# Half loads for the first batch, a fourth early tile, and a new order of the first slots in an attention and mixture-of-experts kernel

## The chip, the cores and the metric

The kernel runs on one core of a Trainium2 chip. TensorE (PE) does the matrix products, ScalarE (ACT) and VectorE (DVE) work on the results, GpSimd (POOL) does part of the element-wise work and starts the indirect transfers, and SyncE (SP) starts the other transfers. Each engine takes its instructions in the order of its own queue, and the engines meet in semaphores. The metric is the device time of one execution in microseconds (us), the median of several runs.

## The reference

Attention over eight batches with eight heads of 64: 32 global tokens that see everything, and 512 local tokens that see the global ones and a window of 32 to either side. Its output, 8 x 544 = 4352 rows of 512, goes through a layer of eight experts, of which each row uses one:

```python
s_ll = np.where(np.abs(pos[:, None] - pos[None, :]) <= 32, s_ll, -1e9)
a_l = sm(np.concatenate([s_lg, s_ll], axis=-1))       # softmax; global queries see all keys
x = attn_out.transpose(0, 2, 1, 3).reshape(4352, 512)
...
e_idx = np.argmax(x @ w_gate, axis=1)                 # one expert for each row
for e in range(8):
    h = np.maximum(x[e_idx == e] @ w1[e], 0.0)        # 512 -> 1024
    out[e_idx == e] = gate_w * eom * (h @ w2[e])      # 1024 -> 512
```

## The kernel before

**Attention.** Each batch has ten units of work: four pairs of heads times two halves of the local rows (`Local`), and two units for the global rows (`Global`) at places 4 and 7. `advance` runs them as a software pipeline: scores of one unit, transposes of the one two places earlier, and the weighted sum (`pv`) of the one three places earlier stand next to each other in the engines' queues. A half's units use the first or the second half of the queries' and keys' columns alone; the global units use all. The queries (32 + 512 columns for each pair) and keys (640 columns, with copies of the global keys between the blocks) are loaded by `load_pairs` (L121 to L125) in pairs of heads on SP's queue; for batch 0 pair 0, then pair 1, then three of the five blocks of values (`load_v`), then pairs 2 and 3, then the other two blocks. The values are split into a high and a low part (`split_v`) after the second and third unit, and `copy_v` copies some of their rows within the on-chip memory on the same SP queue. The mask comes on GpSimd's queue (L158), behind four `memset`s and the identity. Two kinds of units use it: one adds it on VectorE (L272), the other on TensorE (L261).

**Routing.** Each row tile of 128 tokens is split, transposed on SP's queue, and multiplied with the router's weights; `Router.small` then works out expert, rank and weight of each row, and the rows are written to `xd` in DRAM. After the last batch the table is made: how many tiles each expert needs (`tiles`, `cum`), which rows each slot takes (`idx`), and in `tab`, for each slot, whether the expert changes and which weights come next. A slot is 128 rows of one expert; at most NSLOT = 34 + 7 = 41 are needed.

**Early tiles.** KPRE = 3 tiles of expert 0 are taken ahead of the table, from the tokens of the first 25 row tiles (`list_pre`, `fetch_pre`, `turn_pre`). Their 48 chunks of matmuls (8 of stage 1 and 8 of stage 2 for each) are handed out by `work(n)` between the small instructions of the last routing, and `work_all` issues what is left when the table has been made. Each output goes through ScalarE (`s2_out`, L682) and by an indirect transfer on GpSimd (L683) to its rows of `out`.

**Slots.** NBASE = 36 slots always run, and `rest` runs two and three more if slot 36, and then slot 38, is in use. A slot has its rows gathered (`gather`, L1040, GpSimd) and transposed (`xtrans`, L1046, SP), then stage 1 (`stage1`, 96 matmuls of 128 x 128 x 128, L668), the rectifier and split of its result (`between`, L674 and L675, ScalarE and VectorE), stage 2 (24 matmuls of 512 columns, L679) and `store`. `run` works with stage 1 two slots ahead of stage 2. The weights w1 and w2 of an expert (2 MB each) are loaded by `fetch` (L1012, L1014, SP) under a condition from `tab`, and split into high and low halves by ScalarE and VectorE (L693 and L695 for w1). Whether a split is due is decided on the chip: `change` (L1019) and `changes` (L1028) load a flag (L994) and go through a `Switch`, whose arms are real branches of ScalarE's and VectorE's programs. An arm with no split only raises the semaphores. `changes(s)` has w2 of slot s + 1 and w1 of slot s + 3 in its charge. TensorE waits for these semaphores ahead of the next stage 1.

The order of ScalarE, VectorE, TensorE and SP is that of the program text; GpSimd's instructions are placed by a scheduler, except those called through `gp`. The first slots before the change:

```python
for s in range(2):
    change(s, 1)
    stage1(s)
    between(s)
xtrans(3)
changes(-1)
run(0, NBASE)
```

Of the kernel before, what the change touches and what calls it, by code (L numbers as in the profile page):

```python
# [25 lines left out]
P = 128  # L26
NT = NTOK // P
RPE = NT
KPRE = 3
G0, G1 = (4, 7)  # L30
LAG = 4
HK = 1
# [9 lines left out]
FI = (1, 1, 1, 2, 1, 1, 0)  # L42
PART = (0, 16, 31, NT)
NSLOT = NT + E - 1
NBASE = NSLOT - 5
XG = DM + 8
XROW = DM + 16
W = 224
# [10 lines left out]
def tile_attention_moe(  # L59
# [59 lines left out]
    w2l = [base[0][:, 2048 + 256 * f:2304 + 256 * f].bitcast(F16) for f in range(8)]  # L119


    def load_pairs(b, lo, hi):
        _, _, q, k = sets[b % 2]
        nc.sync.dma_start(q[:, lo:hi], qT[b, :, lo:hi])
        nc.sync.dma_start(k[:, lo:hi, 32:KW - 32], kT[b, :, lo:hi])  # L125

    raw = {}

    def load_v(b, i):
        raw[i] = ld.tile([P, VW], F32, name="vf", bufs=5)  # L130
        nc.sync.dma_start(raw[i], vD[b, :, i])

    def split_v(b, i):
# [9 lines left out]
    def copy_v(b, lo=0, hi=3):  # L143
        for t in sets[b % 2][0:2]:
            nc.sync.dma_start(t[0:64, 5 + lo:5 + hi], t[64:128, lo:hi])
            nc.sync.dma_start(t[64:96, 5 + lo:5 + hi], t[64:96, 4:5].broadcast_to([32, hi - lo, VW]))

    for _, _, _, k in sets:
        for lo in (0, KW - 32):
            nc.gpsimd.memset(k[:, :, lo:lo + 32], 0.0)  # L150
# [3 lines left out]
    make_identity(nc, ident)  # L154
    identb = const.tile([P, P], BF16, name="identb")
    nc.vector.tensor_copy(identb, ident)
    mask = const.tile([P, 3, W], BF16, name="mask")
    nc.gpsimd.dma_start(mask, c_mask)  # L158
    load_pairs(0, 0, 1)
    load_pairs(0, 1, 2)  # L160
    for i in (0, 4, 1):
        load_v(0, i)
    load_pairs(0, 2, 4)
    for i in (2, 3):
        load_v(0, i)
    pgbuf = [ld.tile([P, 608], F32, name=f"pgbuf{i}") for i in range(2)]
# [566 lines left out]

    def fetch_pre():
        for t in range(KPRE):
            x = ld.tile([P, XROW], F32, name="kf", bufs=3)
            gp.indirect_dma_start(out=x, out_offset=None, in_=xd[0:1 + NPRE * P, :],
                                         in_offset=bass.IndirectOffsetOnAxis(ap=ixp[:, t:t + 1], axis=0))
            pre[t] = {"x": x}
        pre_at.append(n)  # L740

    def turn_pre():
        for t in range(KPRE):
            xT = ld.tile([P, S], F32, name="qf", bufs=3).bitcast(F16)[:, 0:2 * DM].rearrange("p (k t) -> p k t", t=P)
            nc.sync.dma_start_transpose(out=xT, in_=pre[t]["x"].bitcast(F16)[:, 0:2 * DM])
            pre[t]["xT"] = xT

# [21 lines left out]

    def pre2_out(t):  # L770
        d = pre[t]
        y = ld.tile([P, VW], F32, name="vf", bufs=5)[:, 0:DM]
        s2_out(d["py"], y, d["x"])


# [290 lines left out]
    def run(lo, hi, grouped=True):  # L1066

        for s in range(lo, hi):
# [12 lines left out]
                between(s + 2)  # L1081
            store(s, grouped)

    for s in range(5):
        gather(s)
    for s in range(2):
        xtrans(s)
    fetch(-1, 1)
    fetch(-1, 2)
    xtrans(2)  # L1090
    for s in range(2):
        change(s, 1)
        stage1(s)
        between(s)
    xtrans(3)
    changes(-1)
    run(0, NBASE)

    def rest(lo, sizes):
        if not sizes:  # L1100
            return
        hi = lo + sizes[0]
        more = {e: entry(x, 3, lo) for e, x in ((ET.PE, nc.tensor), (ET.Activation, nc.scalar), (ET.DVE, nc.vector),
                                                (ET.Pool, nc.gpsimd), (ET.SP, nc.sync))}
        for arm in tc.Switch(more, 2):
            if arm == 1:
                for s in range(lo, hi):
                    gather(s)
                for s in range(lo, hi):
                    xtrans(s)  # L1110
                for s in (lo, lo + 1):
                    change(s, 1)
                    stage1(s)
                    between(s)
                if hi > lo + 2:
                    changes(lo - 1)
                else:
                    change(lo, 2)
                run(lo, hi, False)
                rest(hi, sizes[1:])  # L1120

    rest(NBASE, [2, 3])


# [72 lines left out]
```

## Time and profile before

| What | Value |
|---|---|
| Median of 3 runs | 746.26 us (745.1 to 753.59) |
| Profiled execution, device time | 746.95 us |
| Its span, first to last instruction | 745.1 us |
| TensorE busy | 686.4 us (92%) |
| VectorE, ScalarE, GpSimd busy | 51%, 51%, 32% |
| Mean granted TensorE clock | 0.974 |

The profile is of one execution. Busy time is the time in which an engine had an instruction under way. The times in the rows of the timeline count from the first instruction. `L668` is line 668 of the kernel. A `q` behind an engine's name marks its sequencer: flags, branches, semaphores and starts of transfers. The 1.9 us between device time and span lie outside the instructions.

### The profile page before, as it was taken

How to read it: one execution, taken by the hardware profiler on the slowest of the kernel's cores; microseconds unless marked ns; L12 is line 12 of the kernel's file. 1: busy time of each engine (PE TensorE's matmuls, PEld its weight loads, DVE VectorE, ACT ScalarE, POOL GpSimd, SP SyncE). 2: the span in 40 equal slices, each digit the busy share in tenths (PEclk: the TensorE clock that was granted, in tenths of full speed). 3: DMA queues.
4: the chain of work that ended last, by engine and by line, in shares of the span. 5: the costliest groups of instructions: out<-in, count | busy, mean ns of one | idle time of the engine just before them, and what ended most of it. 6: DMA issues, size and time to landing. Idle time of an engine off the chain costs nothing.

```text
span 745.1 us, 23135 instructions
## 1 busy us (share of the span) xinstructions
PE 686.4 (92%) x9042; PEld 525.4 (71%) x9042; DVE 379.4 (51%) x1110; ACT 377.3 (51%) x866; POOL 240.4 (32%) x335
## 2 busy tenths in 40 slices
PE   4999999999999989947999899999999998999991
PEld 3788887878788777647667577667776775776660
DVE  3798989898998976710333410134225251343200
ACT  3788889898899994101342411133235262243210
POOL 3335374664748464320112121111211212121110
PEclk9999999999999999978999999999999999999996
DMA  7764979678677784297548573365765978652110
GB/s 229 226 168 127 293 213 287 148 243 208 161 236 157 208 159 75 101 264 144 168 141 221 112 149 90 81 173 124 166 189 124 238 170 212 163 113 65 49 44 14
DMA packets 113797, 120.18 MB, mean 161 GB/s; under 512 B 81615, under 2 KB 83407, under 8 KB 111762
## 3 DMA queue, kind: packets, MB, share of 16 engines
q1 hardware_dynamic: 106898, 96.85, 51.2%
q0 software_dynamic: 6528, 19.67, 9.2%
q14 instruction: 295, 2.42, 1.2%
q8 instruction: 76, 1.25, 0.7%
HBM read 200.50 MB, written 19.42 MB: 295 GB/s over the span
## 4 chain that ended last, share of the span: by engine, by line
issue 47%; PE 27%; POOL 10%; DVE 8%; ACT 4%; DMA 1%; SPq 1%; POOLq 1%; DVEq 0%; ACTq 0%
PE sp L256 6%; POOL out_dram L683 5%; POOL qkv L1040 4%; PE pt L303 3%; PE pt L308 3%; PE sp L365 2%; DVE dl L324 2%; PE sp L668 1%; DMA qkv<-in_kT_dram 1%; DVE nm L267 1%; PE pt L394 1%; DVE fl L316 1%; PE sp L261 1%; PE po L421 1%; ACT qkv L709 1%
## 5 line engine op out<-in xcount | busy, mean ns | idle before, releaser
L668 PE MATMUL ph<-qkv,w1h 128*128 128x128 f16 x2304 | 203.9, 222 | 15.1 <-DMA qkv<-qkv 10.0
L668 PEld LDWEIGHTS <-w1h 128*128 128x128 f16 x2496 | 197.0, 100 | 24.0 <-issue 10.5
L668 PE MATMUL ph<-qkv,w1l 128*128 128x128 f16 x1152 | 200.8, 222 | 9.3 <-DVEq L1028 4.1
L679 PE MATMUL py<-qkv 128*128 128x512 f16 x864 | 192.0, 379 | 0.0
L675 DVE SCALAR_TENSOR_TENSOR qkv<-ph,qkv 128x512 f16<-128x512 f32 x72 | 46.8, 687 | 213.1 <-ACT qkv L674 120.6
L679 PEld LDWEIGHTS <-qkv 128*128 128x128 f16 x896 | 86.0, 98 | 97.1
L668 PEld LDWEIGHTS <-w1l 128*128 128x128 f16 x1248 | 124.2, 99 | 10.7 <-DVEq L1028 4.6
L674 ACT ACTIVATE qkv<-ph 128x512 f16<-128x512 f32 x72 | 40.0, 594 | 167.0 <-PE ph L668 103.5
L683 POOL DMA_INDIRECT out_dram<-qkv x36 | 36.4, 1011 | 208.5 <-ACT qkv L682 207.5
L1040 POOL DMA_INDIRECT qkv<-xd,idx x36 | 36.5, 1015 | 134.7 <-DMA out_dram<-qkv 131.3
L256 PE MATMUL sp<-qkv 64*128 64x224 f32 x512 | 68.6, 388 | 9.6 <-DMA qkv<-in_kT_dram 9.6
L256 PEld LDWEIGHTS sp<-qkv 64*128 64x128 f32 x512 | 45.6, 193 | 13.5 <-issue 6.3
L285 ACT ACTIVATE p<-p,nb 128x224 f32<-128x224 f32 x128 | 51.0, 474 | 7.3 <-DVE nb L272 7.2
L682 ACT ACTIVATE qkv<-py,qkv 128x512 f32<-128x512 f32 x36 | 24.8, 689 | 58.5 <-PE py L679 39.4
L324 DVE SCALAR_TENSOR_TENSOR dl<-pt,dh 128x512 f16<-128x512 f32 x80 | 53.4, 667 | 0.3
L695 DVE SCALAR_TENSOR_TENSOR w1l<-w1r,w1h 128x512 f16<-128x512 f32 x56 | 34.3, 686 | 37.4 <-ACT w1h L693 34.7
L699 ACT ACTIVATE qkv<-qkv 128x512 f16<-128x512 f32 x56 | 34.6, 629 | 32.5 <-PE py L679 31.7
L701 DVE SCALAR_TENSOR_TENSOR qkv<-qkv 128x512 f16<-128x512 f32 x56 | 34.7, 687 | 30.8 <-ACT qkv L699 21.8
L83 POOL TENSOR_TENSOR xr<-xt,xr 128x512 f16<-128x512 f32 x30 | 34.8, 1160 | 48.0 <-ACT xr L446 36.9
L272 DVE CUSTOM_DVE_ANT_0 p<-sp,mask 128x224 f32<-128x224 f32 x128 | 42.2, 385 | 15.3 <-PE sp L256 6.2
L335 PE MATMUL po<-qkv,fh 96*128 96x65 f16 x256 | 48.1, 196 | 1.1 <-DVE s L548 0.8
L312 ACT ACTIVATE fh<-pt 96x512 f16<-96x512 f32 x64 | 37.7, 589 | 22.1 <-PE pt L303 21.5
(195 smaller groups left out, 1493.5 us busy)
## 6 DMA issues: line engine op xcount, KB each, us to landing
w1r<-in_w_dram SPq DMA_DIRECT2D x38, 2048.0 KB
qkv<-in_w_dram SPq DMA_DIRECT2D x38, 2048.0 KB
vf<-in_vD_dram SPq DMA_DIRECT2D x40, 260.0 KB
qkv<-in_kT_dram SPq DMA_DIRECT2D x7, 1280.0 KB
qkv<-in_qT_dram SPq DMA_DIRECT2D x7, 1088.0 KB
xd<-xr SPq DMA_DIRECT2D x6, 1056.0 KB
qkv<-qkv SPq DMA_DIRECT2D x14, 195.0 KB
xd<-xr SPq DMA_DIRECT2D x4, 528.0 KB
```

Source lines behind the costliest of these rows:

```text
L256: nc.tensor.matmul(self.sp[:, 2 * hd + bi, 0:W], lhsT=self.q[hs, pr, qs], rhs=self.k[hs, pr, ks], start=(bi == 0 or self.fused), stop=self ...
L272: nc.vector.tensor_tensor_reduce(self.p[:, n], self.sp[:, n, 0:W], mask[:, self.half + n % 2], -0.125, 3e38, ALU.add, ALU.min, self.nb[:, ...
L285: nc.scalar.activation(self.p[:, n], src, AF.Exp, bias=self.nb[:, n:n + 1], scale=sc)
L312: nc.scalar.mul(self.fh[0:96], self.pF[0:96], PS)
L324: nc.vector.scalar_tensor_tensor(self.dl, self.pD, PS, self.dh, ALU.mult, ALU.subtract)
L335: nc.tensor.matmul(o, lhsT=fh, rhs=self.vh[0:96, 4 + i, hc], start=True, stop=False)
L668: nc.tensor.matmul(o, lhsT=w[:, k], rhs=xT[:, x], start=(n == 0), stop=(n == 11))
L674: nc.scalar.activation(hh[:, gs], v, AF.Relu)
L675: nc.vector.scalar_tensor_tensor(hl[:, gs], v, 0.0, hh[:, gs], ALU.max, ALU.subtract)
L679: nc.tensor.matmul(py, lhsT=h[:, f], rhs=w, start=(f == 0 and n == 0), stop=(f == 7 and n == 2))
L683: i = nc.gpsimd.indirect_dma_start(out=out[:, :], out_offset=bass.IndirectOffsetOnAxis(ap=x[:, XG:XG + 1].bitcast(U32), axis=0), in_=y, in ...
L1040: nc.gpsimd.indirect_dma_start(out=xs, out_offset=None, in_=xd[:, :], in_offset=bass.IndirectOffsetOnAxis(ap=idx[:, s + 1:s + 2], axis=0))
```

## The change

There are three parts.

1. The mask's load becomes GpSimd's first instruction. Batch 0's queries and keys are loaded in halves of their columns: the first halves of pair 0, pair 1 and pairs 2 and 3 (288 of 544 query columns, 352 of 640 key columns), then three blocks of values, then the second halves of all pairs in one load each, then the other two blocks.
2. KPRE becomes 4, and NBASE becomes 41 - 6 = 35, with two further groups of 3 in `rest`. The rows of the early tiles take buffers of the ring `vf` (five, used before for values and then for early outputs), which are made 528 columns wide; their transposed forms take four buffers of `qf`.
3. `begin` sets the order of the first slots: `change(1)` stands ahead of `between(0)`, and `changes(-1)` ahead of `between(1)`. Slot 2's transpose stands ahead of the first two weight loads.

```diff
-KPRE = 3
+KPRE = 4
-NBASE = NSLOT - 5
+NBASE = NSLOT - 6
...
-    def load_pairs(b, lo, hi):
+    def load_pairs(b, lo, hi, half=None):
+
         _, _, q, k = sets[b % 2]
-        nc.sync.dma_start(q[:, lo:hi], qT[b, :, lo:hi])
-        nc.sync.dma_start(k[:, lo:hi, 32:KW - 32], kT[b, :, lo:hi])
+        a, z = (0, SG + SL) if half is None else ((0, SG + 256), (SG + 256, SG + SL))[half]
+        nc.sync.dma_start(q[:, lo:hi, a:z], qT[b, :, lo:hi, a:z])
+        a, z = (0, KW - 64) if half is None else ((0, 352), (352, KW - 64))[half]
+        nc.sync.dma_start(k[:, lo:hi, 32 + a:32 + z], kT[b, :, lo:hi, a:z])
...
+    mask = const.tile([P, 3, W], BF16, name="mask")
+    nc.gpsimd.dma_start(mask, c_mask)
     for _, _, _, k in sets:
...
-    mask = const.tile([P, 3, W], BF16, name="mask")
-    nc.gpsimd.dma_start(mask, c_mask)
-    load_pairs(0, 0, 1)
-    load_pairs(0, 1, 2)
+    load_pairs(0, 0, 1, 0)
+    load_pairs(0, 1, 2, 0)
+    load_pairs(0, 2, 4, 0)
     for i in (0, 4, 1):
         load_v(0, i)
-    load_pairs(0, 2, 4)
+    load_pairs(0, 0, 4, 1)
...
-            x = ld.tile([P, XROW], F32, name="kf", bufs=3)
+            x = ld.tile([P, XROW], F32, name="vf", bufs=5)
...
-            xT = ld.tile([P, S], F32, name="qf", bufs=3).bitcast(F16)[:, 0:2 * DM].rearrange("p (k t) -> p k t", t=P)
+            xT = ld.tile([P, S], F32, name="qf", bufs=KPRE).bitcast(F16)[:, 0:2 * DM].rearrange("p (k t) -> p k t", t=P)
...
+    def begin(lo, more=True):
+
+        change(lo, 1)
+        stage1(lo)
+        change(lo + 1, 1)
+        between(lo)
+        stage1(lo + 1)
+        if lo == 0:
+            xtrans(3)
+        if more:
+            changes(lo - 1)
+        else:
+            change(lo, 2)
+        between(lo + 1)
+
     for s in range(5):
         gather(s)
-    for s in range(2):
+    for s in range(3):
         xtrans(s)
     fetch(-1, 1)
     fetch(-1, 2)
-    xtrans(2)
-    for s in range(2):
-        change(s, 1)
-        stage1(s)
-        between(s)
-    xtrans(3)
-    changes(-1)
+    begin(0)
     run(0, NBASE)
...
-    rest(NBASE, [2, 3])
+    rest(NBASE, [3, 3])
```

More of the change, by code (lines that the diff above doesn't have):

```diff
@@ L119, in tile_attention_moe @@
     w2l = [base[0][:, 2048 + 256 * f:2304 + 256 * f].bitcast(F16) for f in range(8)]
-    def load_pairs(b, lo, hi):
+    def load_pairs(b, lo, hi, half=None):
         _, _, q, k = sets[b % 2]
-        nc.sync.dma_start(q[:, lo:hi], qT[b, :, lo:hi])
-        nc.sync.dma_start(k[:, lo:hi, 32:KW - 32], kT[b, :, lo:hi])
+        a, z = (0, SG + SL) if half is None else ((0, SG + 256), (SG + 256, SG + SL))[half]
+        nc.sync.dma_start(q[:, lo:hi, a:z], qT[b, :, lo:hi, a:z])
+        a, z = (0, KW - 64) if half is None else ((0, 352), (352, KW - 64))[half]
+        nc.sync.dma_start(k[:, lo:hi, 32 + a:32 + z], kT[b, :, lo:hi, a:z])
     raw = {}
     def load_v(b, i):
-        raw[i] = ld.tile([P, VW], F32, name="vf", bufs=5)
+        raw[i] = ld.tile([P, XROW], F32, name="vf", bufs=5)[:, 0:VW]
         nc.sync.dma_start(raw[i], vD[b, :, i])
@@ L771, in pre2_out @@
         d = pre[t]
-        y = ld.tile([P, VW], F32, name="vf", bufs=5)[:, 0:DM]
+        y = ld.tile([P, XROW], F32, name="vf", bufs=5)[:, 0:DM]
         s2_out(d["py"], y, d["x"])
@@ L1110, in rest @@
                     xtrans(s)
[L1111 to L1118, printed above, removed]
+                begin(lo, hi > lo + 2)
                 run(lo, hi, False)
                 rest(hi, sizes[1:])
-    rest(NBASE, [2, 3])
+    rest(NBASE, [3, 3])
 def _constants():
```

## The prediction

> **What bounds the kernel now.** I read the page first, then stretches of time around the change of phase, then TensorE's timeline, and last the sequencers of the engines that it waited for.
>
> ```profile
> span 745.1 us, 23135 instructions
> PE   4999999999999989947999899999999998999991
> L675 DVE SCALAR_TENSOR_TENSOR qkv<-ph,qkv 128x512 f16<-128x512 f32 x72 | 46.8, 687 | 213.1 <-ACT qkv L674 120.6
> L1040 POOL DMA_INDIRECT qkv<-xd,idx x36 | 36.5, 1015 | 134.7 <-DMA out_dram<-qkv 131.3
> ```
>
> TensorE is full in nearly all forty slices (18.6 us each). The exceptions are the first slice, the slices around 316 to 350 us, and the last. The gather runs 36 times, so 36 slots of the base list are worked, and `rest` is not entered.
>
> ```profile
> core 0: us, PE busy (x) PEld busy (x) DVE busy (x) ACT busy (x) POOL busy (x), PEclk, DMA share, GB/s
> 316.60:326.60 10.00, 0.00 (x2) 0.03 (x2) 0.93 (x6) 0.69 (x1) 5.59 (x6) 0.71 1.01 180
> 326.60:334.24 7.64, 7.63 (x96) 7.46 (x96) 0.69 (x1) 0.60 (x1) 0.00 (x0) 0.71 0.99 356
> 345.69:353.83 8.14, 8.14 (x96) 8.08 (x97) 0.00 (x0) 1.12 (x3) 0.00 (x0) 0.64 0.25 41
> 353.83:364.37 10.54, 10.54 (x123) 7.71 (x121) 6.19 (x10) 4.80 (x10) 1.00 (x1) 1.00 0.41 136
> ```
>
> The columns after the stretch are its length, each engine's busy time, the granted clock, and DMA. Between the phases TensorE stands still for 10.0 us, and the next stage 1 takes 7.64 us at a granted clock of 0.71. The last row is one slot at full clock, stage 2 and the next stage 1: 10.54 us, all of it TensorE.
>
> ```profile
> 316.22 0.38 PE L679 MATMUL pt<-qkv,hl 128*128 128x512 f16 x1
> 326.60 0.37 PE L668 MATMUL ph<-qkv,w1h 128*128 128x128 f16 x2 [10.00 <-DMA qkv<-qkv]
> 335.64 0.28 PE L668 MATMUL ph<-qkv,w1h 128*128 128x128 f16 x2 [1.40 <-ACTq L1019]
> 336.51 0.23 PE L668 MATMUL ph<-qkv,w1l 128*128 128x128 f16 x1 [0.59 <-DVEq L1019]
> 345.69 0.40 PE L668 MATMUL ph<-qkv,w1h 128*128 128x128 f16 x2 [3.75 <-ACTq L1028]
> 353.83 5.34 PE L679 MATMUL py<-qkv 128*128 128x512 f16 x24
> 364.37 0.38 PE L679 MATMUL py<-qkv 128*128 128x512 f16 x1
> ```
>
> Start, length, instruction, and in brackets the idle time with its end. The early tiles end at 316.60. Stage 1 of slot 0 waits until 326.60 for its transposed rows. Stage 1 of slots 1 and 2 start at 335.64 and 345.69, each after a wait on a `Switch` (L1019 in `change`, L1028 in `changes`) that ScalarE and VectorE go through. The first stage 2 starts at 353.83. I count the gain of the middle at that point, since from there one slot follows the other.
>
> **A slot becomes an early tile.** I counted the reference's routing on its inputs: 665, 280, 1086, 535, 312, 321, 617 and 536 tokens, with 596 of expert 0 in the first 25 row tiles. With three early tiles (384 rows) the rest needs 3+3+9+5+3+3+5+5 = 36 slots, as the x36 shows. With four (512 rows, all filled from the 596) expert 0 needs 2, so 35, which is the new NBASE exactly. One slot goes: **-10.54**. The same matmuls come back as 16 chunks after the 48 that are there; the table's instructions stay between the same chunk numbers, so the new work runs at the end, in the hole of 10.00 us. TensorE is done with it at 316.60 + 10.54 = 327.1 where it idled until 326.60. VectorE gets one more `hl` (0.69 us, the 687 ns of L675) ahead of the table's last fields; SP waits for its rows then, so I cost it at nothing.
>
> The fourth tile also adds a fetch on GpSimd and a transpose on SP's queue during the last batch:
>
> ```profile
> 264.63 1.13 POOL L83 DMA_INDIRECT kf<-xd,ixp  x1 [0.17 <-DVE rc L298]
> 268.12 5.14 SPq L745 DMA_TRANSPOSE qf<-kf  x3
> L668 PE MATMUL sp<-qf,w1h x192: 216/219/221, 277.3 to 304.3; 128*128 128x128 f16 x192
> ```
>
> That is about 1.1 us on GpSimd and 5.14 / 3 = 1.7 us on SP. The early tiles are first used at 277.3, and the router's transposes behind it feed TensorE only four units later. I take 0, with bounds 0 and +1.7.
>
> **The new order at the first slots.** What stands ahead of slot 0's stage 1 on ScalarE changes: the output of the last early tile now comes at 327.3 instead of 316.64, and ScalarE's `change(0)` is queued behind it. The prices are in these rows, the last three views being instructions of ScalarE's sequencer (start in us at the end):
>
> ```profile
> 316.64 0.69 ACT L682 ACTIVATE vf<-pt,kf 128x512 f32<-128x512 f32 x1 [5.91 <-PE pt L679]
> 334.27 0.60 ACT L674 ACTIVATE qkv<-ph 128x512 f16<-128x512 f32 x1 [2.03 <-PE ph L668]
> 352.71 4.27 ACT L693 ACTIVATE w1h<-w1r 128x512 f16<-128x512 f32 x8 [10.14 <-PE ph L668]
> 353.83 4.91 DVE L695 SCALAR_TENSOR_TENSOR w1l<-w1r,w1h 128x512 f16<-128x512 f32 x8 [10.01 <-ACT w1h L693]
> L994 ACTq TENSOR_LOAD <-tab x1: 285/285/285, 334.3 to 334.3; - x1
> L1019 ACTq EVENT_SEMAPHORE  x1: 17/17/17, 335.6 to 335.6; - x1
> L994 ACTq TENSOR_LOAD <-tab x1: 287/287/287, 342.0 to 342.0; - x1
> L1028 ACTq EVENT_SEMAPHORE  x1: 17/17/17, 345.6 to 345.6; - x1
> L994 ACTq TENSOR_LOAD <-tab x1: 288/288/288, 348.7 to 348.7; - x1
> ```
>
> A `Switch` costs 1.3 us from the load of its flag to the semaphore in its arm (334.3 to 335.6) or 3.6 (342.0 to 345.6), and 3.1 more to get out to the next load (345.6 to 348.7). With the short price, stage 1 of slot 0 starts at 327.3 + 1.3 = 328.6; I take 329.0 (the wait below included) and 334.3 for its end: stage 1 feeds as many columns as stage 2 (96 x 128 = 24 x 512), so half a slot, 5.3 us at full clock. `change(1)` now stands ahead of slot 0's results: 329 + 3.1 + 1.3 = 333.4, or 335.7 with the long price, so stage 1 of slot 1 starts at some 334.7 and ends at 340.0. The 2.0 us of wait at 334.24 mostly go.
>
> Then `changes(-1)`, ahead of slot 1's results, does real work for the first time: slot 2 is now expert 1's first, so w1 has to be split there. ScalarE leaves `change(1)` at 336.5 to 338.8, does slot 0's results (0.6 until the last has started), goes through the third `Switch` (338.4 to 343.0), and 1.12 + 0.69 us later the first pair of pieces is ready: 340.2 to 344.8. The pieces follow at 4.91 / 8 = 0.61 us, faster than stage 1 uses them (5.3 / 8 = 0.66). I take 341.5, nearer the short end because both L1019 rows were short; then the first stage 2 starts at 346.8 against 353.83: **-7.0**. The bounds are -10.8 (TensorE never waits: 327.1 + 3 x 5.3 = 343.0) and 0 (341.5 becomes 345.7 and the clock falls again).
>
> Two things behind this:
>
> ```profile
> 315.12 1.01 POOL L1040 DMA_INDIRECT qkv<-xd,idx  x1 [1.92 <-issue]
> 320.19 1.01 POOL L683 DMA_INDIRECT out_dram<-vf,kf  x1 [0.30 <-issue]
> out_dram<-vf,kf POOLq DMA_INDIRECT x3, 3.9
> 318.60 4.86 SPq L1046 DMA_TRANSPOSE qkv<-qkv  x2
> 325.55 0.42 SPq L1012 DMA_DIRECT2D w1r<-in_w_dram  x1
> 327.98 10.12 SPq L1046 DMA_TRANSPOSE qkv<-qkv  x1
> ```
>
> The fourth early output reuses the buffer of the third tile's rows, which the third store still reads; that store can be issued at some 322.9 and lands 3.9 us later, at 326.8, or later under load. I cost it at 0.4, with bounds 0 and 2. On SP, slot 2's transpose moves ahead of the two weight loads: it no longer sits 10.12 us behind them, and they start some 3.5 us later than 325.55. Before, both loads (4 MB) were through the queue at 338.1, so now at 341.6 at the latest; w1 is the first of the two, so I expect it before 338, ahead of the split.
>
> **The start.**
>
> ```profile
> 8.76 0.39 DVE L272 CUSTOM_DVE_ANT_0 p<-sp,mask 128x224 f32<-128x224 f32 x1 [5.74 <-DMA mask<-in_c_mask_dram]
> 8.92 1.87 PE L256 MATMUL sp<-qkv 64*128 64x224 f32 x8 [2.70 <-DMA qkv<-in_kT_dram]
> 14.05 1.86 PE L256 MATMUL sp<-qkv 64*128 64x224 f32 x8 [2.50 <-DMA qkv<-in_kT_dram]
> 16.91 0.54 SPq L146 DMA_DIRECT2D qkv<-qkv  x1
> 19.89 0.20 PE L335 MATMUL po<-qkv,fh 96*128 96x65 f16 x1
> 2.00:6.00 4.00, 1.64 (x8) 1.27 (x8) 0.40 (x1) 0.01 (x1) 2.57 (x18) 1.00 0.94 267
> ```
>
> The first units wait for the mask until 8.76 and for keys until 8.92 and 14.05; by the shapes the third unit's keys come at the end of 3.1 MB. By halves they come at the end of 1.28 MB, some 5 us at 267 GB/s, so keys and mask come in time. But the same bytes have to arrive before the copies of the values (issued until 16.91), which queue behind the halves and gate the first weighted sum at 19.89. I take **-2.0**, with bounds 0 (the copies come no sooner) and -5.2 (both key waits, 2.70 + 2.50, carried to the end). A rule speaks against this part: the Trainium skill (DMA: Bandwidth & Descriptors, Measured) wants DMAs of at least 1 MiB and gives 138 GB/s at 64 KB. Pieces of 144 to 352 KB would by it load more slowly, and the term would be 0; the loads of the first pair, 272 and 320 KB by their shapes, make the 267 GB/s above, well over its low figure.
>
> **Sum:** -10.5 - 7.0 - 2.0 = -19.5. The profiled execution took 746.95 us (span 745.1), 0.7 over the median of 746.26; against the median this gives 746.26 - 19.5 = **727**. A measurement of this kernel can tell about 2% (14.9 us) from no change.
>
> **The rivals.**
> (a) No new wait: the `Switch` chain runs under TensorE's work. For it speak the short L1019 rows, against it the 3.6 us of L1028. -10.5 - 10.8 - 2.0 gives 723. By the Trainium skill (Advanced Engine Details and Errata, Control Flow Timing) a compare-and-branch takes about 108 ns, which would favour this; the 3.6 us row disagrees, and Runtime: NRT & Kernel Launch, Instruction fetch mechanics, says that a taken branch out of the fetched window stalls for a fetch, with which that row agrees.
> (b) The new waits take the gap's place: three dispatches at the long price, or w1 late, so the first stage 2 stays at 353.8. Only the slot and the start are won: 746.3 - 12.5 = 734.
> (c) Slower: GpSimd's order puts the gathers behind the store of the fourth tile. That store ends at about 329.3; from gather to first matmul it takes 326.60 - 315.12 = 11.5 us, so slot 0 starts at 340.8, 14.2 late: -10.5 - 2.0 + 14.2 gives 748. It decides as soon as slot 0's gather is behind that store. Against it: before, four gathers went ahead of the third store (320.19).
> (d) The change doesn't do what it says: 36 slots are still needed and `rest` is entered. 35 + 3 slots, two more than before (+21.1), and a new fill of 11.5 give over 770. By the counts no expert is nearer to another slot than 24 tokens.
>
> **How the numbers follow.** My forecast has 0.55, (a) 0.20, (b) 0.19, (c) 0.04, (d) 0.02. The range of 719.5 to 736 holds the forecast and (a) with the start's bounds (723 less 3.2) and (b) with the 1.7 us of the last batch; what it leaves out is (c), (d) and the edges, about 0.1. Faster by over 2% (under 731.3) is the forecast but for 0.02, (a), and 0.02 of (b): 0.75. Slower is (d) and a worse (c): 0.03. The rest, 0.22, is within 2%.
>
> **What would show it.** Right: 35 gathers in slots and four early stores; no 10 us hole at the phase change, a granted clock of 1.0 through the first stage 1; the first stage 2 some 30 us after the old end of the early tiles, with w1's split ending its waits; slot 0 released by ScalarE's `Switch`. Wrong: a wait over 5 us at stage 1 of slot 2 on the load of w1; a gather behind the fourth store; the first weighted sum no earlier than 19.9; or a lasting loss in the last batch.

## The result, and the profile after

| What | Before | After |
|---|---|---|
| Median of 20 runs each | 746.67 us (741.57 to 754.49) | 742.75 us (737.4 to 747.17) |
| Profiled execution: device time, span | 746.95, 745.1 us | 737.4, 735.6 us |
| End of the early tiles on TensorE | 316.60 us | 325.20 us |
| Start of the first stage 2 | 353.83 us | 358.32 us |

The time after is 0.9945 of the time before (95% interval 0.9924 to 0.9966): some 4 us won where the forecast was 19.5. The profiled execution of the changed kernel happens to be the fastest of its twenty, so the 9.5 us between the two profiles aren't the gain.

From the page of the changed kernel (span, TensorE's busy tenths, and two groups):

```profile
span 735.6 us, 23090 instructions
PE   6999999999999989994999999999999998999991
L679 DVE SCALAR_TENSOR_TENSOR qkv<-ph,qkv 128x512 f16<-128x512 f32 x70 | 45.3, 686 | 206.9 <-issue 104.7
L1044 POOL DMA_INDIRECT qkv<-xd,idx x35 | 35.2, 1007 | 134.5 <-DMA out_dram<-qkv 131.0
```

35 gathers: one slot is gone, and `rest` isn't entered. TensorE's dip at the change of phase is one slice later and as deep, and it is narrower: a single 4 where 4, 7 and 8 stood. By stretches of time, cut at the ends of TensorE's waits (length, busy time of each engine, granted clock, DMA):

```profile
core 0: us, PE busy (x) PEld busy (x) DVE busy (x) ACT busy (x) POOL busy (x), PEclk, DMA share, GB/s
325.20:326.88 1.68, 0.00 (x1) 0.00 (x1) 0.00 (x0) 0.69 (x1) 0.62 (x1) 1.00 0.94 255
326.88:338.67 11.79, 5.53 (x96) 5.36 (x96) 0.00 (x0) 0.00 (x0) 0.36 (x1) 0.88 1.04 360
338.67:348.75 10.08, 7.37 (x96) 7.20 (x97) 1.29 (x2) 1.77 (x4) 0.00 (x0) 0.81 0.63 107
348.75:358.32 9.57, 8.38 (x96) 8.21 (x97) 6.19 (x10) 5.15 (x10) 0.00 (x0) 0.64 0.27 85
```

The hole of 10.00 us is down to 1.68. But three stages 1, which would be 16 us of work at full clock, take from 326.88 to 358.32, 31.4 us (before 27.2, from 326.60 to 353.83). 10.2 of these are waits, and 21.3 are TensorE's own work: stage 1 takes 5.53 us in the second row, but 7.37 and 8.38 in the last two, where the granted clock is 0.81 and 0.64. In the second row TensorE works for 5.53 of 11.79 us while ScalarE and VectorE have nothing under way at all. TensorE's timeline names what it waited for:

```profile
326.88 0.29 PE L672 MATMUL ph<-qkv,w1h 128*128 128x128 f16 x2 [1.68 <-ACTq L1023]
338.67 0.39 PE L672 MATMUL ph<-qkv,w1h 128*128 128x128 f16 x2 [6.26 <-ACTq L1023]
348.75 0.29 PE L672 MATMUL ph<-qkv,w1h 128*128 128x128 f16 x2 [2.71 <-ACT w1h L697]
350.23 0.29 PE L672 MATMUL ph<-qkv,w1l 128*128 128x128 f16 x1 [1.19 <-DVE w1l L699]
```

The first row is a wait that was forecast (there 1.5 to 1.9 us, here 1.68). The second is new: 6.26 us ahead of slot 1's stage 1, on the `Switch` of `change(1)` (L1023). ScalarE's sequencer shows why. These are single instructions in order of time, start in us at the end of each row. L998 loads a dispatch's flag, the hint stands at the entry of the arm, L678 is slot 0's results, and the last row is `changes(-1)` at the entry of the arm that splits w1:

```profile
L998 ACTq TENSOR_LOAD <-tab x1: 468/468/468, 325.3 to 325.3; - x1
L1023 ACTq EVENT_SEMAPHORE  x1: 17/17/17, 326.8 to 326.8; - x1
L998 ACTq TENSOR_LOAD <-tab x1: 283/283/283, 333.6 to 333.6; - x1
L1023 ACTq BRANCH_PREFETCH_HINT  x1: 35/35/35, 338.5 to 338.5; - x1
L1023 ACTq EVENT_SEMAPHORE  x1: 17/17/17, 338.6 to 338.6; - x1
L678 ACTq EVENT_SEMAPHORE  x1: 38/38/38, 344.3 to 344.3; - x1
L998 ACTq TENSOR_LOAD <-tab x1: 289/289/289, 344.5 to 344.5; - x1
L1032 ACTq BRANCH_PREFETCH_HINT  x1: 35/35/35, 347.8 to 347.8; - x1
```

The first dispatch takes 1.5 us to its semaphore (325.3 to 326.8), and then 6.8 until the next load (333.6). The second takes 5.0 (333.6 to 338.6) and 5.7 to get out (344.3). The third takes 3.3 to its arm (344.5 to 347.8). In nearly all of these 22.5 us ScalarE does no work: it is on its way from one place of its program to another.

The start of the kernel did better than forecast. Mask-using unit, second unit's scores and first weighted sum of the changed kernel:

```profile
5.83 0.39 DVE L276 CUSTOM_DVE_ANT_0 p<-sp,mask 128x224 f32<-128x224 f32 x1 [2.23 <-PE sp L260]
6.25 1.86 PE L260 MATMUL sp<-qkv 64*128 64x224 f32 x8 [0.46 <-DMA qkv<-in_kT_dram]
16.94 0.20 PE L339 MATMUL po<-qkv,fh 96*128 96x65 f16 x1
```

They stood at 8.76, 8.92 and 19.89: the first weighted sum is 2.95 us earlier. This is no chance of two profiles: in the eleven profiles of this case with the half loads it comes at 16.83 to 18.26, in the three without (before, e6, e11) at 19.89 to 21.65. Part of it is lost again ahead of the phase change. The same stretch of the program, of before and then of after (columns as above):

```profile
255.00:316.60 61.60, 57.22 (x845) 43.78 (x845) 44.41 (x190) 33.40 (x79) 32.86 (x46) 0.97 0.53 118
```

```profile
252.20:325.20 73.00, 67.70 (x965) 51.39 (x965) 48.34 (x197) 35.33 (x82) 39.55 (x53) 0.98 0.62 132
```

TensorE's idle time in it is 61.60 - 57.22 = 4.38 us before and 73.00 - 67.70 = 5.30 after.

### The profile page after: what moved, and what is told of

It is laid out like the page before. It is cut to its first block, busy times and chain, and to the rows that moved or that the text cites. A ratio compares the mean times of both kernels' runs of the same rounds, so it can differ in the third digit from the quotient of the medians.

```text
span 735.6 us, 23090 instructions
## 1 busy us (share of the span) xinstructions
PE 684.9 (93%) x9042; PEld 523.6 (71%) x9042; DVE 380.9 (52%) x1110; ACT 375.7 (51%) x866; POOL 241.2 (33%) x336
## 4 chain that ended last, share of the span: by engine, by line
issue 47%; PE 24%; POOL 11%; DVE 9%; ACT 3%; DMA 2%; POOLq 1%; SPq 0%; DVEq 0%; ACTq 0%
PE sp L260 5%; POOL out_dram L687 5%; POOL qkv L1044 4%; PE pt L307 3%; PE pt L312 2%; DMA xT<-xr 2%; DVE dl L328 1%; PE sp L369 1%; DVE nm L271 1%; PE sp L672 1%; DVE fl L320 1%; POOL qkv L83 1%; PE pt L398 1%; PE sp L265 1%; PE po L425 1%
## 5 line engine op out<-in xcount | busy, mean ns | idle before, releaser
L672 PE MATMUL ph<-qkv,w1h 128*128 128x128 f16 x2240 | 196.8, 222 | 10.9 <-ACTq L1023 7.9
L672 PE MATMUL ph<-qkv,w1l 128*128 128x128 f16 x1120 | 193.9, 222 | 7.5 <-DVE w1l L699 3.4
L683 PE MATMUL py<-qkv 128*128 128x512 f16 x840 | 186.7, 379 | 0.0
L679 DVE SCALAR_TENSOR_TENSOR qkv<-ph,qkv 128x512 f16<-128x512 f32 x70 | 45.3, 686 | 206.9 <-issue 104.7
L683 PEld LDWEIGHTS <-qkv 128*128 128x128 f16 x872 | 83.8, 98 | 94.3
L678 ACT ACTIVATE qkv<-ph 128x512 f16<-128x512 f32 x70 | 38.7, 594 | 148.6 <-PE ph L672 76.9
L703 ACT ACTIVATE qkv<-qkv 128x512 f16<-128x512 f32 x56 | 32.8, 624 | 36.1 <-PE py L683 26.3
L341 PE MATMUL po<-qkv,fl 96*128 96x65 f16 x256 | 48.0, 193 | 0.5 <-DVE fl L320 0.5
```

The lines of the kernel that those rows point to most:

```text
L341: nc.tensor.matmul(o, lhsT=fl, rhs=self.vh[0:96, 4 + i, hc], start=False, stop=False)
L672: nc.tensor.matmul(o, lhsT=w[:, k], rhs=xT[:, x], start=(n == 0), stop=(n == 11))
L678: nc.scalar.activation(hh[:, gs], v, AF.Relu)
L679: nc.vector.scalar_tensor_tensor(hl[:, gs], v, 0.0, hh[:, gs], ALU.max, ALU.subtract)
L683: nc.tensor.matmul(py, lhsT=h[:, f], rhs=w, start=(f == 0 and n == 0), stop=(f == 7 and n == 2))
```

## The experiments

**Theories.** T1: the time went into ScalarE's chain of dispatches, in which each jump costs several us; before, the 10 us hole had covered the first of them. T2: it went into the order of `begin`, which puts `change(1)` ahead of slot 0's results. T3: the weights' streams (4 MB) are what delays the chain, by w1 arriving late or by slowing ScalarE's way. All ratios are to the kernel before on the same chip, with 95% intervals; "gap" is the time from the end of the early tiles to the first stage 2 in the profiled execution (before 37.2, after 33.1).

| Run | Median us | Ratio | Early tiles end | First stage 2 | Gap |
|---|---|---|---|---|---|
| e1 changed kernel again | 741.73 | 0.9883 (0.9838 to 0.9928) | 325.71 | 354.69 | 29.0 |
| e2 old order, four tiles | 744.55 | 0.9936 (0.9883 to 0.9988) | 326.44 | 360.32 | 33.9 |
| e3 no dispatch for slots 0, 1 | 733.1 | 0.9768 (0.9724 to 0.9812) | 326.13 | 346.39 | 20.3 |
| e4 w2's load late | 740.32 | 0.9874 (0.9824 to 0.9923) | 325.54 | 351.48 | 25.9 |
| e5 start only | 744.45 | 0.9955 (0.9925 to 0.9984) | 313.60 | 351.97 | 38.4 |
| e6 order only, three tiles | 743.1 | 0.9953 (0.9923 to 0.9984) | 317.28 | 349.19 | 31.9 |
| e7 first dispatch earlier | 736.8 | 0.9875 (0.9842 to 0.9909) | 325.69 | 353.52 | 27.8 |
| e8 that, and w2 late | 735.97 | 0.9889 (0.9845 to 0.9933) | 326.51 | 349.42 | 22.9 |
| e9 first dispatch twice | 750.38 | 1.0031 (0.9995 to 1.0068) | 324.71 | 363.41 | 38.7 |
| e10 e8, and w1 ahead of transposes | 739.57 | 0.989 (0.9818 to 0.9962) | 325.60 | 350.81 | 25.2 |
| e11 kernel before again | 749.26 | one run | 315.41 | 350.32 | 34.9 |
| e12 two slots for expert 0 | 735.46 | 0.9799 (0.9747 to 0.9851) | 326.96 | 348.61 | 21.6 |

**e1: the changed kernel again**, no edit.

> The changed kernel once more, for a second profile and a ratio on the chip of the runs below. Its profile had the early tiles end at 325.2 and the first stage 2 start at 358.3, 33.1 us later (before: 316.6 and 353.8, 37.2 later). Theory A (ScalarE goes through three dispatches in a row after the last early output, and each stalls for the fetch of its code): again 30 to 36 us between the two, with two or three waits of TensorE on L1023 and the split of w1 in it. Theory D (the profile was a lucky execution and the gain is lost somewhere else): that distance is near 33 but another stretch is longer by some 5 us. Ratio to the kernel before 0.99 to 1.00 by both.

The first stage 2 came at 354.69, 3.6 us sooner than in the first profile: slot 1's wait is 5.78 and slot 2's 0.69. The second dispatch's way out took 4.4 us here, 5.7 there. The gap of 29.0 us is just under the 30 to 36 that were expected. Of the 4.1 us between the two gaps, 1.75 come ahead of slot 2's stage 1 and 2.39 in it: it took 7.18 us here at a granted clock of 1.00, 9.57 there at 0.64. So one kernel's gap varies by some 4 us.

**e2: the old order of the first slots with four early tiles.**

```diff
-    for s in range(3):
-        xtrans(s)
+    for s in range(2):
+        xtrans(s)
     fetch(-1, 1)
     fetch(-1, 2)
-    begin(0)
+    xtrans(2)
+    for s in range(2):
+        change(s, 1)
+        stage1(s)
+        between(s)
+    xtrans(3)
+    changes(-1)
```

> The changed kernel with the order of the first slots of before: slot 2's transpose behind the weight loads, change(1) behind slot 0's results, changes(-1) behind slot 1's. The fourth early tile and the half loads stay. Theory A: the dispatches are the same three and stand on ScalarE one after the other in both orders, so the first stage 2 comes 30 to 36 us after the early tiles' end, within 3 us of the changed kernel, and the time is within 0.5% of it. Rival B (the new order itself costs the gain, by putting dispatches ahead of results that TensorE's next stage waits for nothing of): the distance falls to 25 us or less and the time by 8 us.

The gap is 33.9 us, against 33.1 and 29.0 with the new order, and the ratio's interval overlaps that of the change. T2 falls: with four tiles the chain begins only when the last early output is out, in either order, and the order has little say.

**e3: no dispatch ahead of the first two slots.** It leaves out the test whether w1 has to be split before slots 0 and 1; their loads stay.

```diff
-        change(lo, 1)
+        (change if lo else fetch)(lo, 1)
         stage1(lo)
-        change(lo + 1, 1)
+        (change if lo else fetch)(lo + 1, 1)
```

> The changed kernel without the two dispatches of change(0) and change(1): the test whether w1 has to be split ahead of slots 0 and 1 is left out (with these inputs it is never due); their conditional loads stay. Theory A: TensorE starts stage 1 of slot 0 when its rows are there, slot 1 follows without a wait, and only changes(-1) is left, so the first stage 2 comes 22 to 26 us after the early tiles' end instead of 33, and the time falls by 7 to 11 us against the changed kernel. Rival C (w1's arrival sets the first split): the distance stays at 31 to 35 us and the time within 2 us.

TensorE's timeline of e3:

```profile
326.96 0.27 PE L672 MATMUL ph<-qkv,w1h 128*128 128x128 f16 x2 [0.83 <-ACT vf L686]
339.70 0.28 PE L672 MATMUL ph<-qkv,w1h 128*128 128x128 f16 x2 [1.87 <-ACT w1h L697]
341.13 0.23 PE L672 MATMUL ph<-qkv,w1l 128*128 128x128 f16 x1 [1.15 <-DVE w1l L699]
346.39 5.34 PE L683 MATMUL py<-qkv 128*128 128x512 f16 x24
```

The three stages 1 by stretches of time (columns as above):

```profile
326.96:339.70 12.74, 10.88 (x192) 10.70 (x192) 1.38 (x2) 1.88 (x4) 0.99 (x1) 1.00 1.07 383
339.70:346.39 6.69, 5.54 (x96) 5.37 (x97) 4.92 (x9) 4.68 (x9) 0.00 (x0) 1.00 0.49 56
```

Behind a first wait of 0.83 us slots 0 and 1 run through. TensorE's work in the three stages 1 is 16.4 us, at a granted clock of 1.00, where it was 21.3. The first stage 2 comes 20.3 us after the early tiles: sooner than the 22 to 26 that were expected, and near the 19.7 of the forecast (346.8 less 327.1), which had the two dispatches at a short price. The time falls by 8.6 us against e1 on the same chip (741.73 to 733.1). T1 holds as far as taking away can show it.

**e4: w2's first load behind slot 3's transpose**, so that 2 MB instead of 4 stream during the chain.

```diff
             xtrans(3)
+            fetch(-1, 2)
...
     fetch(-1, 1)
-    fetch(-1, 2)
```

> The changed kernel with the first load of w2 (2 MB) moved on SP's queue from ahead of the first slots to behind slot 3's transpose. Theory A1 (the dispatches are slow because the code they fetch stands behind 4 MB of weights): the ways out of the arms, 6.7 and 5.7 us in the profile of the changed kernel, and the branch of change(1), 4.1 us, fall to about 3 us each at least for those after some 332 us, so the distance from the early tiles' end to the first stage 2 falls from 33 to 26 to 30 us. Theory A2 (a dispatch costs what it costs, whatever is being moved): 32 to 35 us, and the time within 1 us of the changed kernel.

The second dispatch went faster (branch 3.3 us, way out 3.0; e1: 4.4 and 4.4), the first dispatch's way out did not (5.8, e1 6.1). It ran beside w1's stream here too, so this doesn't speak against T3; the second one's price and the gap of 25.9 us are about what was expected if the streams slow the jumps. But the ratio can't be told from e1's, and a gap varies by some 4 us. So w2's stream is at most a part of the loss.

**e5 and e6: one part alone on the kernel before.** e5 has the mask first and the halves; e6 has the new order with three tiles and 36 slots.

> The kernel before with the first part of the change alone: the mask first, batch 0's queries and keys by halves. In the profile of the changed kernel each unit of the attention started 2.8 to 3.0 us sooner than before up to the last batch. If that comes from this part and lasts, the first weighted sum comes at 17 to 18 us instead of 19.9, the early tiles end at 313.5 to 315 instead of 316.6, and the time falls by 2 to 3 us (ratio 0.996 to 0.997). Rival: the gain is taken back in the last batch or at the table; then the early tiles end at 316 to 317 and the time stays.

> The kernel before (three early tiles, 36 slots, whole loads) with the new order of the first slots alone. Theory A (ScalarE's chain of dispatches is what counts, and it begins with the last early output): with three tiles the chain begins at 316.6, so change(0) and change(1) fall into the hole of 10 us and under stage 1 of slot 0; the waits on L1019 ahead of slot 1 go, the one on L1028 ahead of slot 2 shrinks to under 2 us, and the first stage 2 starts at 345 to 348 instead of 353.8: 5 to 9 us saved. Rival B (the new order by itself is no gain): the first stage 2 starts at 352 to 356 and the time stays within 2 us.

Each is worth about 0.5%, some 3.4 us, by itself: together 0.9%, if they add up, which no run shows; that is between the 0.55% of the whole change's twenty runs and the 1.2% of e1. So the removed slot, 10.54 us of TensorE, shows up almost nowhere in the total. e6 says why, with three tiles:

```profile
325.87 0.37 PE L668 MATMUL ph<-qkv,w1h 128*128 128x128 f16 x2 [8.59 <-DMA qkv<-qkv]
341.63 0.28 PE L668 MATMUL ph<-qkv,w1h 128*128 128x128 f16 x2 [3.64 <-ACTq L1028]
349.19 5.34 PE L679 MATMUL py<-qkv 128*128 128x512 f16 x24
```

Here stage 1 of slots 0 and 1 run in one go. ScalarE went through `change(0)` and on to `change(1)` in the 8.59 us in which TensorE waited for its rows. The hole that the fourth tile fills wasn't free: it held the first dispatch's way out. Even so e6 missed what was expected of it: 349.19 instead of 345 to 348, and some 4 us of time (743.1 against 747.05) instead of 5 to 9, for the third dispatch still made slot 2 wait 3.64 us.

**e7 and e8: the first dispatch moved into the early tiles.** `change(0)` and w1's first load go ahead of the last 15 early chunks (one more buffer in `vf`); e8 also has e4's edit.

```diff
-    work_all()
-    att.close()
+    work(49 - nwork[0])
...
     fetch(-1, 1)
+    change(0, 1)
+    work_all()
+    att.close()
     fetch(-1, 2)
     begin(0)
```

> The changed kernel with change(0) and w1's first load moved ahead of the last 15 chunks of the early tiles (all of the fourth tile's stage 2 and most of the third's), so that ScalarE's first dispatch runs while TensorE works on them, and with six buffers in the ring vf. All tests stay. Theory A: TensorE starts slot 0 without a wait on a dispatch, change(1) follows right after the last early output, and the first stage 2 comes 20 to 26 us after the early tiles' end instead of 29 to 33; the time falls by 4 to 9 us against the changed kernel. Rival (the dispatches' place doesn't matter, their number does): 28 us or more, the time within 2 us.

> e7 with w2's first load behind slot 3's transpose, as in e4. Theory A1 (code fetches wait behind the weights): a further 1 to 3 us between the early tiles' end and the first stage 2. Theory A2: the same as e7 within 1 us.

Both beat the kernel before by a little over 1%. e7's interval lies below that of the change's twenty runs, e8's overlaps it, and neither can be told from e1's. e7's gap of 27.8 us missed the expected 20 to 26 and isn't clear of e1's 29.0; e8's of 22.9 is 4.9 shorter again, where 1 to 3 were expected. In e7 TensorE lost much of the lead again:

```profile
332.64 0.28 PE L672 MATMUL ph<-qkv,w1h 128*128 128x128 f16 x2 [0.66 <-ACTq L1019]
346.20 0.40 PE L672 MATMUL ph<-qkv,w1h 128*128 128x128 f16 x2 [7.05 <-ACT w1h L697]
```

The split of w1 waits for the semaphore of slot 1's conditional load. That load is skipped, but it has its place on SP's queue, and SP reached it only at 345.3, behind slot 0's skipped load (341.6) and w2's (343.2). ScalarE stood at that semaphore from 342.2 to 345.4: 3.2 of the 7.05 us. For the rest of them it was still on its jumps. In e8, with w2 out of the way, slot 2 waits 3.76 us.

**e9: the first dispatch twice.** The opposite of e3: one more `Switch` of the same flag, with its empty arm.

```diff
-        fetch(s, which)
+        if twice:
+            change(s, which)
+        else:
+            fetch(s, which)
...
-        change(lo, 1)
+        change(lo, 1, lo == 0)
```

> The changed kernel with the dispatch of slot 0 (load of the flag, Switch with an empty arm taken) issued twice, one behind the other; nothing else is added. Theory (the gap before the first stage 2 is ScalarE's chain of dispatches, each some 1.5 us from flag to semaphore and 4 to 7 us on the way out): the first stage 2 starts 5 to 9 us after the changed kernel's 354.7 to 358.3, at 360 to 366, and the time goes up by the same 5 to 9 us, to 747 to 751. Rival (the dispatches only look long because ScalarE waits in them for w1, so that one more of them hides in the same wait): the first stage 2 stays at 354 to 359 and the time within 2 us of the changed kernel's.

```profile
338.00 0.39 PE L672 MATMUL ph<-qkv,w1h 128*128 128x128 f16 x2 [13.29 <-ACTq L1023]
346.58 0.28 PE L672 MATMUL ph<-qkv,w1h 128*128 128x128 f16 x2 [0.48 <-ACTq L1023]
355.13 0.29 PE L672 MATMUL ph<-qkv,w1h 128*128 128x128 f16 x2 [3.02 <-ACT w1h L697]
```

One empty dispatch more, and slot 0 waits 13.29 us instead of 1.68; the first stage 2 comes at 363.41, 5.1 to 8.7 later than with one, and the whole gain of the change is gone. With e3 this settles T1: taken away or doubled, the time follows the dispatches.

**e10: w1's load ahead of the first three transposes**, on e8.

```diff
+    fetch(-1, 1)
     for s in range(3):
         xtrans(s)
-    fetch(-1, 1)
     change(0, 1)
```

> The version with the first dispatch ahead of the last early chunks and w2's load late, and with w1's first load now also ahead of the three transposes of the first slots. Theory 1 (the loads of skipped experts and w1's split wait for w1's arrival at 338.9 in that version, and the stream slows ScalarE's way out): w1 arrives by 333, the first stage 2 starts at 345 to 347 instead of 349.4, and the time is 2 to 4 us under that version's 735.97. Theory 2 (ScalarE's two remaining dispatches alone set it, at the same price without the stream): the first stage 2 stays at 349 to 350 and the time within 1 us. Rival (the transposes queue behind 2 MB): slot 0's rows come after the end of the early tiles, TensorE waits for them by a DMA, and the first stage 2 comes later than 351.

```profile
332.09 0.37 PE L672 MATMUL ph<-qkv,w1h 128*128 128x128 f16 x2 [6.49 <-DMA qkv<-qkv]
345.56 0.23 PE L672 MATMUL ph<-qkv,w1l 128*128 128x128 f16 x1 [0.55 <-DVE w1l L699]
350.81 5.34 PE L683 MATMUL py<-qkv 128*128 128x512 f16 x24
```

w1 was there by 332.8, as hoped, but slot 0's rows queued behind it: the rival's DMA wait of 6.49 us. Its price would have put the first stage 2 behind 351; it came at 350.81, for ScalarE got its dispatches done in that wait, and slot 2 waited 0.55 us only. The way out of the second dispatch still took 6.1 us, though w1 was there; the DMA queues still moved 158 GB/s in its first 2.5 us. The ratio is the same as e8's.

**e11: the kernel before again**, no edit.

> The kernel before again, for a second profile. If the parts that the prediction took from one profile are steady, the early tiles end at 316 to 317, the first stage 2 starts at 353 to 355, and ScalarE's ways out of its first three dispatches are again 4.4, 5.4 and 3.0 us. If the way out varies from one execution to the next by more than 1.5 us, the first stage 2 moves with it, and a price read from one row was not safe even for the kernel before.

The ways out of the first three dispatches took 4.3, 5.5 and 3.0 us, within 0.1 of the first profile's 4.4, 5.4 and 3.0. They aren't that steady in general: e5, which changes the start alone, has 5.2, 5.6 and 3.0. The first stage 2 came at 350.32, sooner than the expected 353 to 355, for the early tiles ended 1.2 us earlier, slot 0's rows came 0.9 faster, and the third dispatch's branch took 1.6 instead of 2.8. From there to the end of the last stage 2 it took 380.17 us, in the first profile 374.83: this later stretch moves by 5 us between executions of one kernel, and by 9.8 in the two profiles of the changed one (360.79 and 370.58).

**e12: two slots for expert 0, whatever it has left.** The whole computation. The table gives expert 0 at least two slots, so slots 0 and 1 never need a split, and their dispatches and conditional loads leave the program. NSLOT is 43 for the worst case, the base list still 35.

```diff
-NSLOT = NT + E - 1
-NBASE = NSLOT - 6
+NSLOT = NT + E + 1
+NBASE = NSLOT - 8
...
     red(tiles, gt, axis=AX.X, op=ALU.add)
+    ts(tiles[:, 0:1], tiles[:, 0:1], 2.0, None, op0=ALU.max)
...
-        change(lo, 1)
+        if lo:
+            change(lo, 1)
         stage1(lo)
-        change(lo + 1, 1)
+        if lo:
+            change(lo + 1, 1)
...
-    rest(NBASE, [3, 3])
+    rest(NBASE, [3, 5])
```

and e4's edit.

> The whole computation, with no dispatch ahead of the first two slots: the table now always gives expert 0 two slots, whether it has rows for them or not, so slots 0 and 1 can never need a split of w1, and the Switches and conditional loads of slots 0 and 1 are left out of the program (NSLOT becomes 43 for the worst case; the base list stays at 35 slots, for here expert 0 needs two anyway). w2's first load stands behind slot 3's transpose. Theory (ScalarE's dispatches one behind the other are what the changed kernel lost): stage 1 of slots 0 and 1 follow the early tiles without a wait on ScalarE's sequencer, the first stage 2 starts at 345 to 347 and 18 to 21 us after the early tiles, as in the version without those dispatches, and the time is 731 to 735, at 0.975 to 0.982 of the kernel before. Rival (that version gained by something else, such as the missing work at the semaphores, or the loads that it still issued): the first stage 2 comes after 350 and the time stays at 738 to 743.

```profile
327.79 0.27 PE L672 MATMUL ph<-qkv,w1h 128*128 128x128 f16 x2 [0.82 <-ACT vf L686]
340.94 0.28 PE L672 MATMUL ph<-qkv,w1h 128*128 128x128 f16 x2 [2.27 <-ACT w1h L697]
341.72 0.23 PE L672 MATMUL ph<-qkv,w1l 128*128 128x128 f16 x1 [0.50 <-DVE w1l L699]
348.61 5.34 PE L683 MATMUL py<-qkv 128*128 128x512 f16 x24
```

The dispatches' waits are gone, as in e3, at 0.9799 (0.9747 to 0.9851) of the kernel before: this version is faster than the kernel before. Its interval lies wholly below that of the changed kernel's twenty runs; at its upper end it overlaps e1's, and e4's, which has one of its two edits. The first stage 2 missed its expectation by 1.6 us, because the one dispatch that is left took 6.7 us from its flag to its arm:

```profile
L999 ACTq TENSOR_LOAD <-tab x1: 475/475/475, 333.4 to 333.4; - x1
L1033 ACTq BRANCH_PREFETCH_HINT  x1: 46/46/46, 340.1 to 340.1; - x1
```

## Why the prediction was wrong

**A slot becomes an early tile: right in itself.** 35 slots, 16 more early chunks, no hole of 10 us, slot 0 released by ScalarE's `Switch` at 326.88 (forecast 328.6 to 329.0, which is 326.7 to 327.1 with the early tiles done 1.9 us sooner than taken). From the first stage 2 to the end of the last one, four profiles with 36 slots take 374.83 to 380.17 us, mean 376.4; the ten with 35 take 360.79 to 370.58, mean 367.5. That is 8.9 for the 10.54 of the forecast, with single profiles up to 6.8 us from their mean.

**The fourth output's buffer: 0 instead of 0.4.** The output began at 325.29, 0.09 after its last matmul.

**The start: better than forecast.** -2.95 at the first weighted sum instead of -2.0, within the bounds; 1.4 to 1.9 us of it are left where the early tiles end (325.71 and 325.20 for the forecast's 327.1). By halves the second unit waited 0.46 us for keys, where it had waited 2.70 (8.92 to 6.25 in start); the smaller pieces didn't cost the time that the prediction set against this part. By the rule of the Trainium skill that it weighed (DMA: Bandwidth & Descriptors, Measured) nothing would have been won; the measured 2.95 us decides. The fourth tile's load on the last batch was taken as 0 with an upper bound of 1.7; the 0.9 us of idle time above is of that size, though no run took the tile's fetch and transpose alone. e5 by itself gave 0.45%, about 3.4 us.

**The new order at the first slots: the step that failed.** The forecast was -7.0 at the first stage 2; the two profiles of the changed kernel have +0.9 and +4.5 (354.69 and 358.32 against 353.83), outside the stated bounds of -10.8 to 0. They hold the start's gain too, which the forecast counts by itself: from the end of the early tiles the forecast has 19.7 us to the first stage 2 and the profiles 29.0 and 33.1, so that the term alone is +2.3 and +6.4. That is 9.3 to 13.4 of the 15.8 us by which 727 missed 742.75. The mis-sized terms are the dispatches' prices: "A `Switch` costs 1.3 us from the load of its flag to the semaphore in its arm", "and 3.1 more to get out to the next load", with the short price taken "because both L1019 rows were short".

| Step of the chain | Forecast us | Measured, after | Measured, e1 |
|---|---|---|---|
| `change(0)`: flag to semaphore | 1.3 | 1.5 | 1.7 |
| its way out | 3.1 | 6.8 | 6.1 |
| `change(1)`: flag to semaphore | 1.3 to 3.6 | 5.0 | 5.2 |
| its way out | 3.1 | 5.7 | 4.4 |
| `changes(-1)`: flag to arm | 1.3 to 3.6 | 3.3 | 3.2 |
| Stage 1 of slot 2 | 5.3 | 9.6 | 7.2 |

The last row is a second term that came out too small: it was counted at full clock and with no wait for the pieces. In the changed kernel's first profile it ran at a granted clock of 0.64 and waited 1.19 us for a piece, in e1 at 1.00 with a wait of 1.64. The prediction had the clock's fall in its bound alone.

The trace of before had the warning, in rows that the prediction didn't use. The first dispatch there, of ScalarE's sequencer, the wait for slot 0's results that comes next, and slot 1's results behind the second dispatch:

```profile
L1019 ACTq EVENT_SEMAPHORE  x1: 17/17/17, 318.7 to 318.7; - x1
L674 ACTq EVENT_SEMAPHORE  x1: 8486/8486/8486, 323.1 to 323.1; - x1
L674 ACT ACTIVATE qkv<-ph x2: 597/597/597, 341.0 to 342.0; 128x512 f16<-128x512 f32 x2
```

The way out took 4.4 us, and the second one, from 335.6 to slot 1's results at 341.0 (the last row), up to 5.4; 3.1 was one of the shortest of that trace. Of the 23 ways out from an empty arm there that end at a load or a semaphore, eleven take 2.9 to 3.6 us and twelve 4.1 to 8.8, mean 4.5. They can be sorted by what the DMA queues move meanwhile. These are the first 2.5 us of two ways out of before, of the first two of the changed kernel, and of the second one of e4 (GB/s in the last column):

```profile
345.68:348.18 2.50, 2.50 (x24) 2.44 (x25) 0.00 (x0) 0.00 (x0) 0.00 (x0) 0.50 0.05 13
518.26:520.76 2.50, 2.50 (x17) 1.21 (x15) 0.00 (x0) 0.00 (x0) 0.59 (x1) 1.00 0.87 312
326.89:329.39 2.50, 2.50 (x45) 2.50 (x46) 0.00 (x0) 0.00 (x0) 0.35 (x1) 1.00 1.09 242
338.68:341.18 2.50, 2.50 (x24) 2.50 (x25) 0.00 (x0) 0.00 (x0) 0.00 (x0) 0.50 0.80 278
337.30:339.80 2.50, 2.50 (x29) 2.50 (x30) 0.00 (x0) 0.00 (x0) 0.00 (x0) 0.61 0.02 7
```

They took 3.0, 6.2, 6.7, 5.7 and 3.0 us. Of the 23 of before, the nine at up to 126 GB/s took 2.9 to 3.1 us, the seven at 312 and more 5.6 to 6.5, and those between 3.3 to 8.8; in the changed kernel the fourteen at up to 163 GB/s took 2.8 to 4.1, the eight at 242 and more 5.7 to 7.3. The first row is the one from which the prediction took its 3.1. It read the price where 13 GB/s were moving, and put the chain beside the weights' loads, which by its own reckoning go through the queue until 341.6 at the latest.

The entries could have been sorted too. The 24 into an empty arm (L1019, L1028) split by how long ScalarE had been back in its main program: within 2 us of the last jump, six of six took 1.0 to 3.3 us from branch to arm; later, 14 of 18 took 0.42 to 0.45. The 14 into an arm with a split took 2.4 to 4.3. Both short L1019 rows were of the kind that comes after a long stay. In the new order `change(1)` is reached 0.8 us after the jump out of `change(0)`, and its branch cost 4.1 us, more than any of the six. With 4.4 and 5.4 for the ways out, 3.3 for the second entry and 4.3 for the third, the same chain gives 327.3 + 1.3 + 4.4 + 0.9 + 3.3 + 5.4 + 1.1 + 4.3 + 1.8 + 5.3 = 355.1 (0.9 and 1.1 are the flags' loads with slot 0's results, 1.8 the first pieces): the term would have been about +1. That takes the dearest entry of each group, 3.3 and 4.3. With the groups' medians, 1.2 and 2.8, the sum is 351.5, and with 6.0, the median of before's seven ways out at 312 GB/s and more, for both ways out 353.7. Each of these is far from -7.0.

**The rivals.** (b) had the mechanism, "three dispatches at the long price", with its first stage 2 at 353.8; it was given 0.19. Less the start's 2.0 that is 351.8, so its 734 was too low by a further 2.9 to 6.5 us there, and by what the later slots made of the removed one (8.9 for 10.54). Without the first two dispatches, e3 and e12 stand 20.3 and 21.6 us behind the early tiles: near the forecast's 19.7, and not at (a)'s 15.9. (c) didn't come: the six first gathers went ahead of the fourth store. (d) didn't come either. On w1 the forecast was right: SP was past the wait for its arrival at 337.4, ahead of the split at 348. In e3 and e12 too ScalarE began the split within 0.2 us of entering the arm (338.8 and 340.1): it came behind the last dispatch, and not behind w1.

**What stays open.** That the way out costs more beside DMA traffic is read from the rows: no run changes the traffic alone, and e4, which only moves w2's load, is a single profile. It fits the 4.3 and 4.4 us of the first way out in the two profiles of before, where no weights were moving yet but 181 and 200 GB/s were. It isn't the whole: e10's second way out took 6.1 us at 158 GB/s. The price of an entry stays open too: the one dispatch left in e3 and in e12, into an arm with a split after a long stay, took 5.4 and 5.7 us from its branch, above the 2.4 to 4.3 of before. And the sum of the parts: the means of the profiles give +4.4 at the first stage 2 (356.5 against 352.1) and -8.9 after it, -4.5 together, beside the 4 us of the medians; the later waits that move single profiles by 5 to 10 us weren't taken apart.

## What to carry to other kernels

An idle stretch of the busiest engine can be the cover of another engine's serial chain: before filling it, add up that chain without the cover, at prices sorted by the state in which each step is reached (here what the DMA queues move meanwhile), and not at the shortest row. A run-time branch on an engine that releases the bottleneck is such a chain. Here moving its place (e7 and e8, 0.9875 and 0.9889) gained less than making it needless (e3 and e12, 0.9768 and 0.9799), though e12's interval touches theirs. With two guaranteed slots in the table and w2's load late (e12) the change stands at 0.980 of the kernel before, with w2's load late alone (e4) at 0.987, and without either at 0.9945 in its twenty runs.

## What the runs showed of the hardware

An empty dispatch on ScalarE, whose own instructions are a load and some register work, took 7 to 13 us from its flag to the next instruction of the main program when it followed another in the first slots (7.2 in e4, 5.0 + 5.7 in the changed kernel, 12.6 in e7), and one more of them cost 5.1 to 8.7 us at the first stage 2 (e9). The Trainium skill (Advanced Engine Details and Errata, Control Flow Timing) gives about 108 ns for a compare-and-branch; from the branch to the arm the shortest here took 0.42 us (before) and the longest ahead of a first stage 2 5.99 (e7). Runtime: NRT & Kernel Launch, Instruction fetch mechanics, of the Trainium skill has a taken branch stall for a fetch when its target lies outside the fetched window. The traces agree: in before, ten of the 14 entries of 0.42 to 0.45 us have no packet of the instruction queues that starts in them, and each of the 23 ways out has at least two. They don't say which engine a packet is for.

A way out cost 2.9 to 3.1 us in before while the DMA queues moved up to 126 GB/s, and 5.6 to 6.5 at 312 GB/s and more.

TensorE's 96 matmuls of a stage 1 took 5.54 us at a granted clock of 1.00 (e3), and 8.38 at 0.64 behind the waits of the changed kernel.

A conditional load that is skipped still holds its place and its semaphore on SP's queue. In e7 it kept ScalarE at the head of a split from 342.2 to 345.4, in TensorE's wait of 7.05 us, though w1's stream was over: from 341 to 343 the DMA queues moved 8 GB/s.
